# Softmax sums kept per row, heads of batch 0 moved by a quarter, and filler products between quarters of a decode kernel

## The chip, the core and the metric

The kernel runs on one core of a Trainium2 chip. The core's engines work side by side and wait for each other by semaphores: PE (TensorE, matrix products), DVE (VectorE), ACT (ScalarE), POOL (GpSimd) and SP (SyncE, which here only starts DMA transfers). The metric is the device time of one execution in microseconds, lower is better.

## The reference

One decode step of a transformer block for two sequences: layernorm, attention of one query over the last 2048 positions of a cache of 8192 (32 heads of 192), an output projection, and a gated feed-forward.

```python
q = (x_norm @ wq).reshape(B, 1, 32, 192)            # B = 2, D = 640
k = k_cache[:, :, 8192 - 2048:, :]                  # W = 2048 positions
v = v_cache[:, :, 8192 - 2048:, :]
scores = einsum("bhqd,bhkd->bhqk", q, k) * 192 ** -0.5
p = softmax(scores, axis=-1)
o = einsum("bhqk,bhkd->bhqd", p, v)
h = x + o.reshape(B, 1, 6144) @ wo
out = h + (gelu(norm(h) @ w_gate) * (norm(h) @ w_up)) @ w_down
```

All inputs are bf16. K and V of the window are some 100 of the 122 MB that the kernel reads.

## The kernel before

**Blocks and quarters.** K and V come in eight blocks each: block i holds 512 positions of all 32 heads of one batch, 128 partitions of 48 KB, one row for each head and each run of 128 positions (partition 4 h + r). Four blocks make a batch. A block is worked on as two *quarters* g (16 in all, two for each block, eight for each batch); a quarter is 64 positions of each of the 128 rows. Below, the two quarters of one block are called a pair, counted from 0 to 7.

**Memory.** A ring in SBUF has three slots of 48 KB a partition: two for K (blocks in turn) and one for V. SP issues in one order: wq, K0, V0, K1, V1, K2 and so on, then the four parts of wo and the feed-forward weights. Each issue waits until what lay in its place has been used: V of pair i+1 waits for the last PV product of pair i, and K of pair i+2 stands behind it in SP's queue.

**One pair (loop at the end of the kernel; `emit_loop` writes it as a hardware loop over J of four trips, two pairs a trip).**
- `transposes` (L554): K must lie with the head dimension on partitions. PE transposes 128x128 f32 tiles (two bf16 in one f32) in 12 groups of 4 into four PSUM banks `tps`; 7 groups are copied out by DVE (L565), 5 by ACT (L563).
- `scores` (L615): 24 products of 512 columns into the bank `sps`. Each of the 128 output rows holds the scores of one head and one group of positions; four rows make up a head.
- `row_max` and `softmax`: DVE adds a mask and takes each row's maximum (L625), spreads it by a one-hot row into `mrhs`; PE multiplies by the permutation `pm` (L633) so that each row sees the maxima of the four rows of its head; DVE reduces these to the negated maximum `nms` (L635); ACT takes the exponential with its row sums `zr` (L637).
- `e_blocks`: DVE transposes the weights in 32x32 blocks and places them (L647, L649); `pv`: 64 products with V (L661); DVE copies the result to `osb` (L670).
- The transposes of the second quarter stand in PE's queue before and after the first quarter's L633.
- After two pairs: `weights` (minimum of the stored `nms`, factors `wz` by ACT, L643) and `combine` (PE product with `rowsel`, L678; DVE joins the four `osb` and the older sum into `osum`, L684).
- `heads_done(b)` divides by the sum, spreads `osum` over the columns by f32 products with `colsel` (L695) and brings the heads into the layout for the output projection. For batch 0 it runs inside the loop after J = 1, behind pair 3; for batch 1 after the loop, followed by `oproj` (L718) and the feed-forward.

Every engine takes its instructions in program order. PE's order inside the loop is therefore that of the calls:

```python
                scores(g + 1)
                e_blocks(g)
                row_max()
                softmax(g + 1)
                if g % 4 == 2:
                    weights()
                e_blocks(g + 1)
                pv(g)
                pv(g + 1)
            combine()
            if J == 1:
                P.loop_seg("op", J)
                heads_done(0)
```

Of the kernel before, what the change touches and what calls it, by code (L numbers as in the profile page):

```python
# [6 lines left out]
F32 = mybir.dt.float32  # L7
I32 = mybir.dt.int32
# [219 lines left out]


GRAN = 256  # L230
SLOT = 49152
RING = 3 * SLOT
TPG = 128
# [3 lines left out]
BIG = 1.0e9  # L237
# [9 lines left out]
def bass_sequential_preLN__sliding_block_cached__geglu_ffn__decode_kernel(  # L247
# [12 lines left out]
    with ExitStack() as ctx:  # L260

        def sb(name, shape, dt):
            return ctx.enter_context(nc.sbuf_tensor(name, shape, dt))
# [8 lines left out]
        identf = sb("identf", [128, 128], F32)  # L272
        onesd = sb("onesd", [128, 128], F32)
        pm = sb("pm", [128, 128], BF16)
        rowsel = sb("rowsel", [128, 128], F32)
        colsel = sb("colsel", [128, 512], F32)
        mska = sb("mska", [128, 32], F32)
        oht = sb("oht", [128, 4], F32)
# [7 lines left out]
        pf = sb("pf", [128, 9], F32)  # L286
        pg = sb("pg", [128, 14], F32)
        ci = sb("ci", [128, 128], I32)
        cf = sb("cf", [128, 3, 128], F32)
        ei = sb("ei", [128, 6], I32)  # L290
        ef = sb("ef", [128, 6], F32)
        ge = sb("ge", [128, 6, 5], F32)
# [16 lines left out]
        qrow = sb("qrow", [128, 2, 2, DH], BF16)  # L309
        rq = sb("rq", [128, 6, 4, 32], BF16)  # L310
        qs = sb("qs", [128, 384], BF16)
        mx = sb("mx", [128, 1], F32)
        mrhs = sb("mrhs", [128, 4], BF16)
        sm = sb("sm", [128, 512], F32)
        gate = sb("gate", [128, 1], F32)
        nms = sb("nms", [128, 5], F32)
        nmin = sb("nmin", [128, 1], F32)
        zr = sb("zr", [128, 5], F32)
        z5 = sb("z5", [128, 5], F32)
        wz = sb("wz", [128, 6], F32)  # L320
        wp = sb("wp", [128, 6], F32)
        rinv = sb("rinv", [128, 1], F32)
        eexp = sb("eexp", [128, 512], BF16)
        et = sb("et", [128, 512], BF16)
        eblk = sb("eblk", [128, 2, 16, 4, 32], BF16)
        osb = sb("osb", [128, 4, DH], F32)
        osum = sb("osum", [128, DH], F32)
        onrm = sb("onrm", [128, DH], F32)
        cti = eexp[:, :].bitcast(I32).rearrange("p (k x) -> p k x", k=2)
        cxi = ktr[:, 0, :].bitcast(I32)[:, 0:512]  # L330
        cxf = ktr[:, 1, :].bitcast(F32)[:, 0:512]
        ot32 = sb("ot32", [128, 24], F32)
# [78 lines left out]

        def dve(fn, R=(), W=(), X=(), cls=1):
            return P.op("dve", fn, R, W, X, cls=cls if looped else 0)

        def act(fn, R=(), W=(), X=(), cls=0):
            return P.op("act", fn, R, W, X, cls=cls)

        def pe(fn, R=(), W=(), X=(), cls=0):
            return P.op("pe", fn, R, W, X, cls=cls)

        def pool(fn, R=(), W=(), X=()):
            return P.op("pool", fn, R, W, X)

        def ts(out, in0, s1, op0, s2=None, op1=None):
            def fn(e):
                kw_ = {"op1": op1} if op1 is not None else {}
                return e.tensor_scalar(out=out, in0=in0, scalar1=s1, scalar2=s2, op0=op0, **kw_)  # L427
            return fn
# [73 lines left out]
            k = BITS.index(m)  # L502
            return pf[:, k:k + 1]

        for k, pat in enumerate(([[4, 32], [0, 4]], [[0, 4], [1, 32]])):
            pool(lambda e, k=k, pat=pat: e.iota(cti[:, k, :], pattern=pat, base=0, channel_multiplier=0), W=[("cti", k)])
        pool(lambda e: e.tensor_copy(cf[:, 1:3, :], cti[:, :, :]), R=[("cti", k) for k in range(2)], W=["cfm"])

        pool(ts(pg[:, 4:5], rb(28), rb(96), ALU.add), R=["pf"], W=["p124"])
        pool(ts(pg[:, 5:6], rb(3), rb(12), ALU.add), R=["pf"], W=["p15"])  # L510
# [17 lines left out]
        pool(lambda e: e.memset(osum[:, :], 0.0), W=["osum"])  # L528

        def consts_late():  # L530
            pool(ts(rowsel[:, :], cf[:, 2, :], 4.0, ALU.mult, pg[:, 4:5], ALU.is_equal), R=["cfm", "p124"], W=["rowsel"])
            pool(ts(mask16[:, :], cf[:, 0, 0:16], pg[:, 5:6], ALU.is_equal), R=["cf0", "p15"], W=["mask16"])
            pool(lambda e: e.iota(cxi, pattern=[[1, 32], [0, 16]], base=0, channel_multiplier=0), W=["cxi"], X=["ktrc"])
            pool(lambda e: e.tensor_copy(cxf, cxi), R=["cxi"], W=["cxf"])
            pool(ts(colsel[:, :], cxf, rb(31), ALU.is_equal), R=["cxf", "pf"], W=["colsel"] + [("kt", n) for n in range(12)])
            pool(ts(bsel[:, :], cf[:, 0, 0:2], rb(31), ALU.is_equal, 1.0 / D, ALU.mult), R=["cf0", "pf"], W=["bsel"])
            for h in range(2):
                pool(ts(hsel[:, h, :], cf[:, 0, 0:17], 512.0 * h, ALU.add, pg[:, 12:13], ALU.is_equal), R=["cf0", "c63"], W=[("hsel", h)])
# [81 lines left out]
            if g % 4 == 3 and g + 1 < 4 * NQ:  # L620
                q_masked((g + 1) // 8)

        def row_max():
            dve(lambda e: e.memset(gate[:, :], 0.0), W=["gate"], X=["s"], cls=0)
            dve(lambda e: e.tensor_tensor_reduce(  # L625
                out=sm[:, :].rearrange("p (u x) -> p u x", x=32), in0=sps[:, :].rearrange("p (u x) -> p u x", x=32),
                in1=mska[:, :].unsqueeze(1).to_broadcast([128, 16, 32]), scale=1.0, scalar=-2.0 * BIG, op0=ALU.add, op1=ALU.max,
                accum_out=mx[:, :]), R=["mska"], W=["sm", "mx"], X=["s"], cls=0)
            dve(ts(mrhs[:, :], oht[:, :], mx[:, 0:1], ALU.mult), R=["oht", "mx"], W=["mrhs"], cls=0)

        def softmax(g):
            n = g % 4
            pe(lambda e: e.matmul(m2[:, 256:260], lhsT=pm[:, :], rhs=mrhs[:, :], start=True, stop=True),  # L633
               R=["pm", "mrhs"], X=["m2"])
            dve(lambda e: e.tensor_reduce(out=nms[:, n:n + 1], in_=m2[:, 256:260], axis=AX.X, op=ALU.max, negate=True),  # L635
                W=[("nm", n)], X=["m2"], cls=0)
            act(lambda e: e.activation(out=eexp[:, :], in_=sm[:, :], func=ACT.Exp, bias=nms[:, n:n + 1], scale=1.0,  # L637
                                       accum_out=zr[:, n:n + 1]), R=[("nm", n), "sm", "gate"], W=["eexp", ("zr", n)])

        def weights():  # L640
            dve(lambda e: e.tensor_reduce(out=nmin[:, :], in_=nms[:, :], axis=AX.X, op=ALU.min), R=[("nm", k) for k in range(5)],
                W=["nmin"], cls=0)
            act(lambda e: e.activation(out=wz[:, 0:5], in_=nms[:, :], func=ACT.Exp, bias=nmin[:, 0:1], scale=-1.0),  # L643
                R=["nmin"] + [("nm", k) for k in range(5)], W=["wz"])

        def e_blocks(g):
            dve(lambda e: e.transpose(et[:, :], eexp[:, :]), R=["eexp"], W=["et"], cls=0)  # L647
# [22 lines left out]
            dve(lambda e: e.tensor_copy(osb[:, g % 4, :], bank[:, 0:DH]), W=[("osb", g % 4)], X=[x], cls=0)  # L670

        def combine():
            dve(lambda e: e.tensor_tensor_reduce(out=z5[:, :], in0=wz[:, 0:5], in1=zr[:, :], scale=1.0, scalar=0.0, op0=ALU.mult,
                                                 op1=ALU.add, accum_out=wz[:, 5:6]), R=["wz"] + [("zr", k) for k in range(5)],
                W=["z5", "wz5"], cls=0)
            dve(lambda e: e.tensor_copy(zr[:, 4:5], wz[:, 5:6]), R=["wz5"], W=[("zr", 4)], cls=0)
            dve(lambda e: e.tensor_copy(nms[:, 4:5], nmin[:, :]), R=["nmin"], W=[("nm", 4)], cls=0)
            pe(lambda e: e.matmul(m2[:, 264:270], lhsT=rowsel[:, :], rhs=wz[:, :], start=True, stop=True), R=["rowsel", "wz", "wz5"],  # L678
               X=["m2"])
            dve(lambda e: e.tensor_scalar(out=wp[:, :], in0=m2[:, 264:270], scalar1=0.25, scalar2=None, op0=ALU.mult), W=["wp"],  # L680
                X=["m2"], cls=0)
            dve(ts(osum[:, :], osum[:, :], wp[:, 4:5], ALU.mult), R=["wp", "osum"], W=["osum"], cls=0)
            for k in range(4):
                dve(lambda e, k=k: e.scalar_tensor_tensor(out=osum[:, :], in0=osb[:, k, :], scalar=wp[:, k:k + 1], in1=osum[:, :],  # L684
                                                          op0=ALU.mult, op1=ALU.add), R=["wp", "osum", ("osb", k)], W=["osum"], cls=0)

        def heads_done(b):
            dve(lambda e: e.reciprocal(rinv[:, :], wp[:, 5:6]), R=["wp"], W=["rinv"])
            dve(ts(onrm[:, :], osum[:, :], rinv[:, 0:1], ALU.mult, 0.25, ALU.mult), R=["rinv", "osum"], W=["onrm"])
            dve(lambda e: e.memset(nms[:, 4:5], BIG), W=[("nm", 4)])  # L690
            for y in range(2):
                def fn(e, y=y):
# [44 lines left out]
            pe(fn, R=["hrow", ("hsel", 0), ("hsel", 1)], X=["m2"])  # L737


        consts_late()  # L740
        q_rows()
        q_stationary()
        looped.append(True)
        for J in range(4):
            P.loop_seg("a", J)
            for g in (4 * J, 4 * J + 2):
                transposes(g, 0, 12)
                scores(g)
                row_max()
                transposes(g + 1, 0, 4)  # L750
                softmax(g)
                transposes(g + 1, 4, 12)
                scores(g + 1)
                e_blocks(g)
                row_max()
                softmax(g + 1)
                if g % 4 == 2:
                    weights()
                e_blocks(g + 1)
                pv(g)  # L760
                pv(g + 1)
            combine()
            if J == 1:
                P.loop_seg("op", J)
                heads_done(0)
        P.loop_seg()
        heads_done(1)
        for J in range(4):
# [87 lines left out]
             dma="dout")  # L856


        P.resolve({("dve", 0): 4 * 17 + 10, ("dve", 1): 0, ("dve", 2): 1, ("pe", 2): 1, ("act", 1): 0, ("act", 0): 4 * 6 + 1, ("pool", 0): 4})
        sems = {}  # L860
        for e, c in (("pe", 0), ("pe", 1), ("pe", 2), ("dve", 2), ("act", 0), ("act", 1), ("dve", 0), ("dve", 1), ("pool", 0)):
            sems[e, c] = ctx.enter_context(nc.semaphore(f"s_{e}{c}"))
# [3 lines left out]
        nc.sync.wait_ge(sems["d", "dout"], 16)  # L866
        P.emit("pool", nc.gpsimd, sems)
        P.emit("act", nc.scalar, sems)
        order = ["a", (0, 2, ["op"])]
        P.emit_loop("dve", nc.vector, sems, 4, order)  # L870
        P.emit_loop("pe", nc.tensor, sems, 4, order)

# [27 lines left out]
```

## Time and profile before

| | |
|---|---|
| median of 3 runs | 300.34 us (298.68 to 300.59) |
| profiled execution | 299.82 us, span of its instructions 298.5 us |
| busy: PE, DVE, ACT, POOL | 182.9 us (61%), 154.2 (52%), 93.4 (31%), 22.0 (7%) |
| bytes read from HBM | 122.29 MB, 410 GB/s over the span |
| mean granted PE clock | 0.897 |

The page cuts the span into 40 slices of 7.46 us; a digit is a share in tenths. The granted clock is that share of full speed which PE's clock gate lets through. A line of a timeline gives start, length, engine, line of code, operation, output and inputs, shapes, the count of instructions merged into it, and in brackets the idle time before it with what ended it. A line of the view of stretches gives, for each engine, the busy time and the count of instructions, and at its end the granted clock, the DMA share and GB/s.

### The profile page before, as it was taken

Reading aid. Unit: us, or ns where it says so; the run is one execution under the profiler, and the core shown is the slowest. Engines: PE = TensorE matmul, PEld = TensorE weight load, DVE = VectorE, ACT = ScalarE, POOL = GpSimd, SP = SyncE. Lnnn points to the kernel's source line nnn. Section 1 sums busy time; section 2 is a strip of 40 time slices with the busy share of each in tenths; the row PEclk is TensorE's granted clock in tenths of the full one; section 3 lists DMA queues with packets and bytes.
Section 4 is the critical chain, followed back from the end, with each engine's and each line's share of the span. In section 5 each row is a group of like instructions: output and inputs, shape, how many; then the busy total and the mean of one; then the engine's idle time right before and its main releaser. Section 6 shows DMA issues by size and latency. Waiting matters only on the chain.

```text
span 298.5 us, 6292 instructions
## 1 busy us (share of the span) xinstructions
PE 182.9 (61%) x2573; PEld 148.7 (50%) x2573; DVE 154.2 (52%) x387; ACT 93.4 (31%) x124; POOL 22.0 (7%) x67
## 2 busy tenths in 40 slices
PE   2007088629852985298539864994278628862685
PEld 1006087418732973197338743872277418742352
DVE  5000046735675567256766683667446724676413
ACT  1001036405630563046302550662046404640001
POOL 8910200000020000000200000002000000000000
PEclk9999759997998799869995999799879986999589
DMA  8999999999999999999999998999999989999990
GB/s 317 493 403 417 422 422 422 451 397 448 450 435 411 435 422 429 408 435 428 441 402 422 422 422 336 422 422 422 448 461 441 435 329 415 410 428 432 424 400 32
DMA packets 4203, 122.44 MB, mean 410 GB/s; under 512 B 478, under 2 KB 608, under 8 KB 1248
## 3 DMA queue, kind: packets, MB, share of 16 engines
q1 hardware_dynamic: 4044, 121.90, 96.1%
q10 hardware_dynamic: 148, 0.40, 0.3%
q8 instruction: 7, 0.11, 0.1%
q14 instruction: 4, 0.03, 0.0%
HBM read 122.29 MB, written 0.00 MB: 410 GB/s over the span
## 4 chain that ended last, share of the span: by engine, by line
DMA 55%; PE 24%; DVE 9%; ACT 6%; issue 3%; SPq 1%; DVEq 0%; ACTq 0%
DMA ring<-in_A_k_cache_dram 48%; PE tpp L554 13%; DMA ring<-in_A_wq_dram 7%; ACT ktr L563 4%; DVE eblk L649 2%; PE sps L615 2%; PE m L661 2%; ACT eexp L637 2%; DVE et L647 2%; PE m L718 2%; PE tpp L577 2%; PE sps L695 1%; DVE ktr L565 1%; DVE sm L625 1%; SPq L371 1%
## 5 line engine op out<-in xcount | busy, mean ns | idle before, releaser
L554 PE MATMUL tpp<-identf,ring 128*128 128x128 f32 x768 | 105.5, 303 | 38.4 <-DMA ring<-in_A_k_cache_dram 37.7
L554 PEld LDWEIGHTS tpp<-identf,ring 128*128 128x128 f32 x768 | 97.9, 157 | 46.9 <-DMA ring<-in_A_k_cache_dram 38.8
L563 ACT ACTIVATE ktr<-tpp 128x1024 bf16<-128x1024 bf16 x80 | 77.5, 1026 | 120.9 <-PE tpp L554 120.9
L565 DVE COPY ktr<-tpp 128x1024 bf16<-128x1024 bf16 x112 | 75.3, 689 | 62.5 <-PE tpp L554 61.4
L615 PE MATMUL sps<-ktr,rq 128*32 128x512 bf16 x384 | 25.2, 390 | 13.8 <-DVE ktr L565 13.8
L615 PEld LDWEIGHTS sps<-ktr,rq 128*32 128x32 bf16 x384 | 10.0, 94 | 24.2 <-ACT ktr L563 17.5
L431 POOL TENSOR_TENSOR rq<-qs,mask 128x192 bf16<-128x192 bf16 x16 | 7.7, 514 | 182.3 <-PE sps L615 168.4
L637 ACT ACTIVATE eexp<-sm,nms 128x512 bf16<-128x512 f32 x16 | 11.6, 723 | 29.1 <-DVE nms L635 29.1
L661 PE MATMUL m<-ring,eblk 128*32 128x192 bf16 x512 | 12.2, 248 | 13.3 <-DVE eblk L649 13.3
L649 DVE COPY eblk<-et 32x512 bf16<-32x512 bf16 x64 | 18.2, 285 | 2.1
L661 PEld LDWEIGHTS m<-ring,eblk 128*32 128x32 bf16 x512 | 10.4, 108 | 15.1 <-DVE eblk L649 15.1
L625 DVE CUSTOM_DVE_ANT_1 sm<-sps,mska 128x512 f32<-128x512 f32 x16 | 11.0, 691 | 7.4 <-issue 7.0
L577 PE MATMUL tpp<-ring,xnT 128*32 128x192 bf16 (+1 forms) x112 | 5.2, 371 | 15.4 <-DMA ring<-in_A_wq_dram 15.4
L647 DVE STREAM_TRANSPOSE et<-eexp 128x512 bf16<-128x512 bf16 x16 | 11.3, 706 | 6.3 <-ACT eexp L637 6.3
L577 PEld LDWEIGHTS tpp<-ring,xnT 128*32 128x32 bf16 x112 | 4.1, 133 | 16.2 <-issue 15.5
L661 PE MATMUL ops<-ring,eblk 128*32 128x192 bf16 x512 | 12.2, 248 | 0.0
L600 DVE CAST qs<-ops 128x384 bf16<-128x384 f32 x1 | 0.6, 558 | 21.3 <-PE ops L595 21.3
L695 PE MATMUL sps<-onrm,colsel 128*128 128x192 f32 x16 | 6.6, 566 | 7.3 <-DVE nms L690 6.0
L661 PEld LDWEIGHTS ops<-ring,eblk 128*32 128x32 bf16 x512 | 10.4, 108 | 0.1
L633 PE MATMUL m<-mrhs,pm 128*128 128x4 bf16 x16 | 2.8, 173 | 11.8 <-DVE mrhs L427 11.8
L633 PEld LDWEIGHTS m<-mrhs,pm 128*128 128x128 bf16 x16 | 1.5, 96 | 15.9 <-DVE mrhs L427 15.9
L695 PEld LDWEIGHTS sps<-onrm,colsel 128*128 128x128 f32 x16 | 4.5, 324 | 8.5 <-DVE nms L690 6.1
(131 smaller groups left out, 94.1 us busy)
## 6 DMA issues: line engine op xcount, KB each, us to landing
ring<-in_A_k_cache_dram SPq DMA_DIRECT2D x8, 6144.0 KB, 34.1
ring<-in_A_v_cache_dram SPq DMA_DIRECT2D x8, 6144.0 KB, 20.1
ring<-in_A_wq_dram SPq DMA_DIRECT2D x1, 7680.0 KB, 21.8
ring<-in_A_wo_dram SPq DMA_DIRECT2D x4, 1920.0 KB, 26.6
ring<-in_B_w_gate_dram SPq DMA_DIRECT2D x1, 1536.0 KB, 21.0
ring<-in_B_w_up_dram SPq DMA_DIRECT2D x1, 1536.0 KB, 24.2
ring<-in_B_w_down_dram SPq DMA_DIRECT2D x1, 960.0 KB, 19.8
ring<-in_B_w_down_dram SPq DMA_DIRECT2D x1, 480.0 KB, 20.6
```

The lines of the kernel that those rows point to most:

```text
L431: return lambda e: e.tensor_tensor(out=out, in0=a, in1=b, op=op)
L554: ins = e.transpose(bank[:, 128 * u:128 * (u + 1)], kv[:, off:off + 128], identf[:, :])
L563: act(lambda e, dst=dst, src=src: e.activation(out=dst, in_=src, func=ACT.Copy), W=[("kt", n)], X=[x])
L565: dve(lambda e, dst=dst, src=src: e.tensor_copy(dst, src), W=[("kt", n)], X=[x], cls=0)
L577: ins = e.matmul(tps[0][32 * r:32 * (r + 1), u:u + n], lhsT=xnT[:, c, 32 * J:32 * (J + 1)], rhs=wq[:, c, o:o + n], start=(c == 0 and J == ...
L615: ins = e.matmul(sps[32 * hg:32 * (hg + 1), :], lhsT=rq[:, k, hg, :], rhs=cols, start=(k == 0), stop=(k == 5), tile_position=(0, 32 * hg))
L625: dve(lambda e: e.tensor_tensor_reduce(out=sm[:, :].rearrange("p (u x) -> p u x", x=32), in0=sps[:, :].rearrange("p (u x) -> p u x", x=32) ...
L637: act(lambda e: e.activation(out=eexp[:, :], in_=sm[:, :], func=ACT.Exp, bias=nms[:, n:n + 1], scale=1.0, accum_out=zr[:, n:n + 1]), R=[(" ...
L647: dve(lambda e: e.transpose(et[:, :], eexp[:, :]), R=["eexp"], W=["et"], cls=0)
L649: dve(lambda e, hg=hg: e.tensor_copy(eblk[32 * hg:32 * (hg + 1), g % 2, :, hg, :], et[32 * hg:32 * (hg + 1), :].rearrange("p (a x) -> p a ...
L661: ins = e.matmul(bank[32 * r:32 * (r + 1), 0:DH], lhsT=eblk[:, g % 2, a, :, :].rearrange("p s x -> p (s x)")[:, r:128:4], rhs=vv[:, DH * t ...
L695: ins = e.matmul(sps[:, DH * j:DH * (j + 1)], lhsT=colsel[:, 128 * J:128 * (J + 1)], rhs=onrm[:, :], start=True, stop=True, skip_group_che ...
```

## The change

Four things are altered.

- **Own maximum and sums for each row.** A quarter's softmax no longer asks for the maximum of its head. DVE negates the masked scores and takes the row's minimum straight into `nms`, and ACT takes the exponential with it. So the rows of a head have different offsets.
- **Rows joined once per two pairs.** `maxima` (before the second quarter's `e_blocks`) takes the smallest `nms` of a row over the quarters and the older sum, and the factors `wz`. `sums` (between the two PV products) multiplies by `pm` for the head's common maximum, gives each row its factor `wz[:, 5]` to it, and joins the sums. `combine` has two PE products, a permutation `rowperm` for the factors and `rowsum` for the sum over the rows of a head.
- **Heads of batch 0.** `heads_done(0)` is called after pair 4 (g = 8) instead of after pair 3. The loop's body has a second part for it, "b".
- **Filler.** `keep_busy` is called once in each pair, after `pv(g + 1)` and `combine`. It issues 11 f32 products of `rowsum` with `sm` (128x512) into the bank `tps[3]`; nothing reads what they write.

```diff
+FILL = 11
...
-        def row_max():
+        def softmax(g):
+            n = g % 4
             dve(lambda e: e.memset(gate[:, :], 0.0), W=["gate"], X=["s"], cls=0)
             dve(lambda e: e.tensor_tensor_reduce(
...
-                in1=mska[:, :].unsqueeze(1).to_broadcast([128, 16, 32]), scale=1.0, scalar=-2.0 * BIG, op0=ALU.add, op1=ALU.max,
-                accum_out=mx[:, :]), R=["mska"], W=["sm", "mx"], X=["s"], cls=0)
-            dve(ts(mrhs[:, :], oht[:, :], mx[:, 0:1], ALU.mult), R=["oht", "mx"], W=["mrhs"], cls=0)
+                in1=mska[:, :].unsqueeze(1).to_broadcast([128, 16, 32]), scale=-1.0, scalar=2.0 * BIG, op0=ALU.add, op1=ALU.min,
+                accum_out=nms[:, n:n + 1]), R=["mska"], W=["sm", ("nm", n)], X=["s"], cls=0)
+            act(lambda e: e.activation(out=eexp[:, :], in_=sm[:, :], func=ACT.Exp, bias=nms[:, n:n + 1], scale=-1.0,
+                                       accum_out=zr[:, n:n + 1]), R=[("nm", n), "sm", "gate"], W=["eexp", ("zr", n)])
+
+        def maxima():
+            dve(lambda e: e.tensor_reduce(out=nmin[:, :], in_=nms[:, :], axis=AX.X, op=ALU.min), R=[("nm", k) for k in range(5)],
+                W=["nmin"], cls=0)
+            dve(ts(mrhs[:, :], oht[:, :], nmin[:, 0:1], ALU.mult), R=["oht", "nmin"], W=["mrhs"], cls=0)
+            act(lambda e: e.activation(out=wz[:, 0:5], in_=nms[:, :], func=ACT.Exp, bias=nmin[:, 0:1], scale=-1.0),
+                R=["nmin"] + [("nm", k) for k in range(5)], W=["wz"])
+
+        def sums():
             pe(lambda e: e.matmul(m2[:, 256:260], lhsT=pm[:, :], rhs=mrhs[:, :], start=True, stop=True),
                R=["pm", "mrhs"], X=["m2"])
...
+            dve(lambda e: e.tensor_reduce(out=nmh[:, :], in_=m2[:, 256:260], axis=AX.X, op=ALU.min), W=["nmh"], X=["m2"], cls=0)
+            act(lambda e: e.activation(out=wz[:, 5:6], in_=nmin[:, :], func=ACT.Exp, bias=nmh[:, 0:1], scale=-1.0),
+                R=["nmin", "nmh"], W=["wz5"])
+            dve(lambda e: e.tensor_tensor_reduce(out=z5[:, :], in0=wz[:, 0:5], in1=zr[:, :], scale=1.0, scalar=0.0, op0=ALU.mult,
+                                                 op1=ALU.add, accum_out=zsum[:, :]), R=["wz"] + [("zr", k) for k in range(5)],
+                W=["z5", "zsum"], cls=0)
+            dve(lambda e: e.tensor_copy(zr[:, 4:5], zsum[:, :]), R=["zsum"], W=[("zr", 4)], cls=0)
+            dve(lambda e: e.tensor_copy(nms[:, 4:5], nmin[:, :]), R=["nmin"], W=[("nm", 4)], cls=0)
+            dve(tt(wz[:, 6:7], wz[:, 5:6], zsum[:, :], ALU.mult), R=["wz5", "zsum"], W=["wz6"], cls=0)
...
         def combine():
...
-            pe(lambda e: e.matmul(m2[:, 264:270], lhsT=rowsel[:, :], rhs=wz[:, :], start=True, stop=True), R=["rowsel", "wz", "wz5"],
-               X=["m2"])
...
+            def fn(e):
+                e.matmul(m2[:, 264:270], lhsT=rowperm[:, :], rhs=wz[:, 0:6], start=True, stop=True)
+                return e.matmul(m2[:, 270:271], lhsT=rowsum[:, :], rhs=wz[:, 6:7], start=True, stop=True)
+
+            pe(fn, R=["rowperm", "rowsum", "wz", "wz5", "wz6"], X=["m2"])
...
+        def keep_busy():
+            def fn(e):
+                for k in range(FILL):
+                    ins = e.matmul(tps[3][:, :], lhsT=rowsum[:, :], rhs=sm[:, :], start=True, stop=True)
+                return ins
+
+            pe(fn, R=["rowsum", "sm"], X=[("t", 3)])
...
                 transposes(g, 0, 12)
                 scores(g)
-                row_max()
-                transposes(g + 1, 0, 4)
                 softmax(g)
-                transposes(g + 1, 4, 12)
+                transposes(g + 1, 0, 12)
                 scores(g + 1)
                 e_blocks(g)
-                row_max()
                 softmax(g + 1)
                 if g % 4 == 2:
-                    weights()
+                    maxima()
                 e_blocks(g + 1)
                 pv(g)
+                if g % 4 == 2:
+                    sums()
                 pv(g + 1)
-            combine()
-            if J == 1:
-                P.loop_seg("op", J)
-                heads_done(0)
+                if g % 4 == 2:
+                    combine()
+                keep_busy()
+                if g == 8:
+                    P.loop_seg("op", J)
+                    heads_done(0)
+                if g % 4 == 0:
+                    P.loop_seg("b", J)
...
-        order = ["a", (0, 2, ["op"])]
+        order = ["a", (1, 3, ["op"]), "b"]
```

`heads_done` itself now scales `osum` by one factor per row, `wfin`, which `combine` has made from `rowsum`'s sum and the row's own factor.

## The prediction

> **What bounds the kernel now.** I read the slices of the page first, then the chain that ended last, then the DMA issues of SP and the PE timeline where a K block lands. The slices:
>
> ```profile
> PEclk9999759997998799869995999799879986999589
> DMA  8999999999999999999999998999999989999990
> GB/s 317 493 403 417 422 422 422 451 397 448 450 435 411 435 422 429 408 435 428 441 402 422 422 422 336 422 422 422 448 461 441 435 329 415 410 428 432 424 400 32
> ```
>
> DMA is busy nearly always, so up to the last block the time is that of moving K and V: 12.6 MB a pair of quarters. K blocks are detected on PE at 67.75, 97.61, 126.68, then 186.21, 217.96 and 247.19. The shortest steps are 29.1 and 29.2 us, the longest 31.7: SP issues the next V only when the pair's last PV product is done (212.4 us of SP's waiting is for L661), and where that came late DMA ran dry. From the timelines of SP and PE:
>
> ```profile
> 183.47 0.54 SPq L371 DMA_DIRECT2D ring<-in_A_v_cache_dram  x1
> ...
> 210.65 0.54 SPq L371 DMA_DIRECT2D ring<-in_A_v_cache_dram  x1
> ...
> 186.21 4.07 PE L554 MATMUL tpp<-identf,ring 128*128 128x128 f32 x20 [2.79 <-DMA ring<-in_A_k_cache_dram]
> ...
> 217.96 4.31 PE L554 MATMUL tpp<-identf,ring 128*128 128x128 f32 x25 [6.30 <-DMA ring<-in_A_k_cache_dram]
> ```
>
> At 183.47 only 2.8 us were left before K landed; the slice around it fell to 336 GB/s and the next K came 31.7 us later. At 210.65, 7.3 us were left and the next step took 29.2. So PE idles 2.8 to 7.3 us between pairs. That idle time is the whole budget of the filler.
>
> One pair takes, from the first transpose to the last PV product, 24.1 us (67.75 to 91.86). I cut it at PE's marks: transposes of the first quarter until its scores 7.8 (67.75 to 75.52), scores 1.5, transposes of the second 6.75 (77.05 to 83.80), scores to the end of PV 8.06. The first part runs at half clock, in the view of stretches:
>
> ```profile
> 67.75:70.60 2.85, 2.85 (x14) 2.85 (x15) 0.69 (x1) 0.85 (x1) 0.00 (x0) 0.50 0.72 310
> 70.60:75.50 4.90, 4.06 (x36) 3.70 (x34) 4.05 (x6) 4.06 (x5) 0.00 (x0) 1.00 1.07 461
> 126.68:132.00 5.32, 5.32 (x25) 5.32 (x26) 2.08 (x3) 2.05 (x2) 0.00 (x0) 0.50 1.00 425
> ```
>
> The third figure from the end is the granted clock. The other pairs begin with 2.8 to 5.3 us at 0.50.
>
> **The filler.** One call is 11 f32 products of 128x512, queued on PE behind the pair's last PV product and ahead of the next pair's first transpose. The trace has no such shape. The nearest rows are the f32 products of L695 and the f32 transposes, each asked for inside one stretch:
>
> ```profile
> L695 PE MATMUL sps<-onrm,colsel x3: 527/527/527, 276.3 to 276.9; 128*128 128x192 f32 x3
> ...
> L554 PE MATMUL tpp<-identf,ring x10: 421/421/421, 68.2 to 70.1; 128*128 128x128 f32 x10
> ...
> L554 PE MATMUL tpp<-identf,ring x15: 272/273/394, 70.4 to 72.0; 128*128 128x128 f32 x15
> ```
>
> L695 stands with 16 records for 8 products in the code, so one f32 product is two records. Their starts lie 0.32 us apart (three starts in 0.6 us) for 192 columns at clock 0.50, that is 1.67 ns a column. The transposes confirm it and show the other clock: 1.9/9 = 0.21 us for 128 columns at 0.50 (1.65 ns a column), 1.6/14 = 0.11 at 1.00, half. So 512 columns cost 0.853 us a record at 0.50 and 0.427 at 1.00. The filler starts right after PV, where the clock stands at 1.00 (it fell only at 94.5, 2.6 us after the last PV record), and is itself dense, so I take 1.00: 22 x 0.427 = **9.4 us a call**, eight calls, 75 us of PE. The ends: with a weight load of 0.188 us (L678's f32 load at full clock) between records 13.5 us; all at half clock 18.8; at one record a product 4.7. The loads of L695 lie beside the products (each starts with the record before it, and 0.337 us of load fits a spacing of 0.32), so I take 9.4.
>
> The Trainium skill, "FP8 and Floating Point Precision", section TensorE Precision Notes, gives true FP32 four passes through the array, which is what two records of two cycles a column amount to. "Perfetto Trace Analysis", section Engine Utilization, halves the array's rate for one FP32 form; by that a call would be 4.7 us. The record count of L695 stands with the first.
>
> **What the filler warms.** The next transposes follow it at once, at full clock. In the first part 2.85 us at 0.21 held 13.4 transposes, which at 0.11 take 1.4 us: about 1.45 us saved. PE then is no longer its limit: seven DVE copies of 0.69 and five ACT copies of 1.02 on four banks give some 6.3 us, the same saving. (The second quarter's transposes, warm, took 6.75 with softmax work between.)
>
> **Own maximum for each row.** Removed per quarter: mrhs (0.23 to 0.53), PE product L633 (0.18), nms reduction (0.16) and their hand-overs. In the second quarter they are on the path:
>
> ```profile
> 86.33 0.08 DVE L625 DVE_READ_ACCUMULATOR2_ANT mx<- 128x1 f32 x1
> 86.45 0.53 DVE L427 TENSOR_SCALAR mrhs<-oht,mx 128x4 bf16<-128x4 f32 x1
> ...
> 87.44 0.72 ACT L637 ACTIVATE eexp<-sm,nms 128x512 bf16<-128x512 f32 x1 [3.82 <-DVE nms L635]
> ```
>
> The exponential moves from 87.44 to about 86.48: 0.96 us saved. In the first quarter it frees nothing: e_blocks still stands behind the last of the seven DVE copies, and the exponential, now ahead of ACT's first copy instead of its third, delays that copy to about 1.7 us after the first transpose (before 1.2); ACT's 0.72 + 5 x 1.0 us ends as before. I add 0.1. Pair: 24.1 - 1.45 - 0.95 + 0.1 = **21.8 us**.
>
> **maxima, sums, combine.** nmin and mrhs (0.16 + 0.23) lie under the exponential (0.72 + 0.19). The small DVE steps of sums (some 0.9 us by the rows of 0.14 to 0.17) lie under the second PV product (1.52). combine now has four f32 PE records instead of two; with weight loads of 0.19 they hold PE 0.7 us ahead of the filler, after pairs 1, 3, 5 and 7. Its DVE work (3 us) lies under the filler. The two added POOL steps (about 1 us) have ended long before the first scores at 46.
>
> **Heads of batch 0.** They move behind the filler of pair 4 (pairs counted from 0). Before, they delayed pair 4: products 155.88 to 159.81, transposes only from 159.60. At full clock I take 2.4 us of PE (two times 0.85, plus 0.57 and hand-overs), plus 1.0 for the DVE steps (0.57 + 0.82 + 0.18) that then stand ahead of the first copies: 3.4 us. The loop's new branches lie under the filler.
>
> **The sum.** Pair 0 starts at 38.25 as before and still cold; its PV ends at 63.1 - 1.0 = 62.1. Each further pair begins when the filler ends, since K lands earlier: at worst the K after next landed 34.5 us after a pair's end before (183.47 to 217.96), while PE now asks for it 9.5 + 21.8 + 9.5 us after. So PE sets the period, 21.8 + 9.5 = 31.3 us against 29.1. Last PV: 62.1 + 7 x 31.3 + 3 x 0.7 + 3.4 = 286.7, before 271.68.
>
> Tail: heads_done(1)'s first product started 4.1 us after the last PV; now 0.7 + 9.4 + 0.1 = 10.2 after, the DVE work being long ready: 296.9. From there the old tail took 22.7 (275.78 to 298.5). At a warm clock two times 0.75 go from the products and perhaps 1.0 from oproj, whose 5.25 us ran at 0.65 on average. 296.9 + 20.2 = 317.1 span. The profiled execution took 299.82 for a span of 298.5, and lay 0.5 under the median of 300.34; with its 1.3 us: **318 us**. With F for one filler, the span is 241.9 + 8 F as long as PE sets the period; it meets the old one at F = 7.1.
>
> **Rivals.**
> - *The filler fits (faster).* One record a product, F = 4.7: the pair is 26.6 us, DMA sets 29.1, no pair comes late again (K of pair 7 at 67.7 + 6 x 29.1 = 242.3 instead of 247.2), last PV 264.1, tail 25.7: span 290, 291 us. For it: the idle time of 4.6 to 7.3 us has room for 4.7. Against it: 16 records for 8 products. It decides wherever F is under 7.1. Chance 0.08.
> - *Near the old time:* pair and filler together about 29 us, each some 1.2 us shorter than I have them: 297 to 303. 0.03.
> - *The weight loads don't overlap* (13.5 a call: 351 us) or the clock is cut to half in the dense products (18.8: 394 us). Against both: L695's loads; no stretch of dense PE work before shows under 1.00 once warm. 0.06 together.
> - The forecast holds 0.83. Its own spread: a filler record by the transposes' warm spacing with its bank waits (0.467) adds 7; a pair 0.8 shorter and nothing for heads and combine takes away 10.
>
> The range 308 to 326 leaves out the rivals. Within 1% is what a measurement here can't tell from no change. Faster 0.09, same 0.03, slower 0.88.
>
> **What would show it.** Right: PE busy without a break from PV to the next transposes, in 22 records spaced 0.43; no PE wait for K after pair 0; granted clock 1.00 from 43 us on; K steps of about 31.5 us; DMA with gaps, under 400 GB/s; SP's V issues at about 62, 93, 125, 156. Wrong: filler records at another spacing (F enters eight times), PE waits for K of some us in each pair, or a pair that isn't 21.8 us because copies, not PE, hold its first part.

## The result and the profile after

The changed kernel takes 325.47 us against 299.86 (medians of six runs each). The ratio is 1.088, with a 95% interval of 1.080 to 1.095; this ratio and those below leave out executions more than 1.5% longer than the fastest of their kernel. The forecast was slower, 318 us, with 308 to 326 as its range. The ratio on the 300.34 us that the forecast started from gives 326.6, just over the range. So the direction and the bound were right and the size was too small: 18 us foretold, 25 to 26 measured. The single executions took 324.0 to 331.7 us at mean granted clocks of 0.963 to 0.937; the shortest has the highest clock, but the order is not strict (325.0 us at 0.945, 326.0 at 0.953). The profiled one is the shortest; its span is 322.6 us against 317.1 foretold.

The slices of the changed kernel's page:

```profile
PE   1015288798869887988798869886998599869685
PEclk9999589999999997999999979999999979999989
DMA  9899999999999996999799979995799979899900
GB/s 372 384 458 404 457 408 453 411 451 420 435 374 392 402 469 281 402 402 463 305 402 390 463 293 396 408 463 219 292 463 414 390 305 475 385 430 422 406 18 2
```

PE's row has risen, and DMA's row has holes, the deepest a slice of 219 GB/s. The chain that ended last says the same by engine, 56% PE and 12% DMA where it was 24% and 55%:

```profile
PE 56%; DVE 13%; DMA 12%; issue 12%; ACT 7%; DVEq 0%; SPq 0%
PE tpp L753 25%; PE tpp L559 22%; DMA ring<-in_A_k_cache_dram 12%; PE m L673 4%; DVE eblk L661 4%; ACT eexp L635 4%; DVE et L659 4%; ACT ktr L568 2%; DVE sm L631 2%; PE m L728 2%; DVE ot L712 1%; PE sps L705 1%; DVE sm L435 1%; DVE ktr L570 0%; PE sps L820 0%
```

L753 is the filler, a quarter of the span on the chain. PE's timeline around the first filler, and SP's issues of V, which mark the ends of pairs 0 to 4:

```profile
62.53 9.71 PE L753 MATMUL tpp<-sm,rowsum 128*128 128x512 f32 x22
72.08 5.51 PE L559 MATMUL tpp<-identf,ring 128*128 128x128 f32 x48
```

```profile
62.64 0.54 SPq L375 DMA_DIRECT2D ring<-in_A_v_cache_dram  x1
...
94.81 0.53 SPq L375 DMA_DIRECT2D ring<-in_A_v_cache_dram  x1
...
127.42 0.53 SPq L375 DMA_DIRECT2D ring<-in_A_v_cache_dram  x1
...
159.52 0.54 SPq L375 DMA_DIRECT2D ring<-in_A_v_cache_dram  x1
...
191.96 0.53 SPq L375 DMA_DIRECT2D ring<-in_A_v_cache_dram  x1
```

22 records hold PE from 62.53 to the next transpose at 72.08, with no idle time in between and no wait for K. The pair's steps are 32.2, 32.6, 32.1 and 32.4 us where 31.3 or 32.0 were foretold.

**Where the rest came from.** The half-clock stretches of the loop have become fewer, but are not gone; they have moved from the start of a pair to its end. The clock fell at 125.31, 190.17 and 258.43 us. In the view of stretches, the 3.41 us ahead of each fall, and after two of them what followed:

```profile
121.90:125.31 3.41, 1.21 (x63) 1.00 (x56) 2.32 (x8) 0.82 (x2) 0.00 (x0) 1.00 1.04 449
124.90:127.30 2.40, 2.37 (x64) 2.08 (x64) 0.36 (x1) 0.00 (x0) 0.00 (x0) 0.59 0.05 21
127.30:129.00 1.70, 1.70 (x7) 0.87 (x4) 0.36 (x1) 0.00 (x0) 0.00 (x0) 0.58 1.01 347
186.76:190.17 3.41, 1.22 (x61) 1.00 (x56) 2.21 (x6) 0.79 (x2) 0.00 (x0) 1.00 1.00 432
255.02:258.43 3.41, 1.22 (x60) 1.22 (x64) 2.21 (x6) 0.12 (x2) 0.00 (x0) 1.00 0.53 231
258.80:262.10 3.30, 3.30 (x8) 1.50 (x5) 0.36 (x1) 0.00 (x0) 0.00 (x0) 0.54 0.71 238
```

The first figure after the length is PE's busy time, the third from the end the granted clock. Ahead of each fall PE was busy 1.2 us of 3.41: the window holds the whole idle time of 2.2 us between the two groups of PV products, and on one or both sides of it some of these products. What followed, PV products and the first filler records, ran at a granted clock of 0.54 to 0.59 on average. PE's timeline for pair 2:

```profile
121.22 1.52 PE L673 MATMUL ops<-ring,eblk 128*32 128x192 bf16 x64 [0.22 <-DVE eblk L661]
124.93 2.46 PE L673 MATMUL m<-ring,eblk 128*32 128x192 bf16 x64 [2.20 <-DVE eblk L661]
127.32 10.39 PE L753 MATMUL tpp<-sm,rowsum 128*128 128x512 f32 x22
```

That is 2.46 us instead of 1.52, and 10.39 instead of 9.71. In the kernel before, the idle time here was 1.67 us, and a window of 3.41 us around it held 1.75 us of PE work; the clock stayed at 1.00. Its timeline in pair 1 and the view of stretches in pair 2:

```profile
90.33 1.52 PE L661 MATMUL m<-ring,eblk 128*32 128x192 bf16 x64 [1.67 <-DVE eblk L649]
```

```profile
118.39:121.80 3.41, 1.75 (x79) 1.34 (x68) 2.10 (x6) 0.00 (x0) 0.00 (x0) 1.00 0.83 360
```

With own maxima the first PV product no longer stands behind L633 and starts earlier (at once after `e_blocks`), so the gap grew by half a microsecond.

### The profile page after: what moved, and what is told of

The parts are those of the page before. It is cut to its first block, busy times and chain, and to the rows that moved or that the text cites. A ratio compares the mean times of both kernels' runs of the same rounds, so it can differ in the third digit from the quotient of the medians.

```text
span 322.6 us, 6609 instructions
## 1 busy us (share of the span) xinstructions
PE 247.5 (77%) x2745; PEld 169.9 (53%) x2745; DVE 151.0 (47%) x373; ACT 94.7 (29%) x128; POOL 22.9 (7%) x69
## 4 chain that ended last, share of the span: by engine, by line
PE 56%; DVE 13%; DMA 12%; issue 12%; ACT 7%; DVEq 0%; SPq 0%
PE tpp L753 25%; PE tpp L559 22%; DMA ring<-in_A_k_cache_dram 12%; PE m L673 4%; DVE eblk L661 4%; ACT eexp L635 4%; DVE et L659 4%; ACT ktr L568 2%; DVE sm L631 2%; PE m L728 2%; DVE ot L712 1%; PE sps L705 1%; DVE sm L435 1%; DVE ktr L570 0%; PE sps L820 0%
## 5 line engine op out<-in xcount | busy, mean ns | idle before, releaser
L570 DVE COPY ktr<-tpp 128x1024 bf16<-128x1024 bf16 x112 | 76.6, 690 | 80.9 <-PE tpp L559 79.6
L568 ACT ACTIVATE ktr<-tpp 128x1024 bf16<-128x1024 bf16 x80 | 76.6, 1018 | 118.9 <-PE tpp L559 118.9
L559 PE MATMUL tpp<-identf,ring 128*128 128x128 f32 x768 | 92.8, 280 | 11.8 <-DMA ring<-in_A_k_cache_dram 8.9
L559 PEld LDWEIGHTS tpp<-identf,ring 128*128 128x128 f32 x768 | 85.7, 143 | 23.0 <-DMA ring<-in_A_k_cache_dram 9.0
L753 PE MATMUL tpp<-sm,rowsum 128*128 128x512 f32 x176 | 80.6, 615 | 0.0
L753 PEld LDWEIGHTS tpp<-sm,rowsum 128*128 128x128 f32 x176 | 34.1, 198 | 41.0 <-issue 40.9
L673 PE MATMUL m<-ring,eblk 128*32 128x192 bf16 x512 | 14.3, 269 | 17.7 <-DVE eblk L661 17.1
L673 PEld LDWEIGHTS m<-ring,eblk 128*32 128x32 bf16 x512 | 11.9, 115 | 19.1 <-DVE eblk L661 18.3
L435 DVE TENSOR_TENSOR sm<-sps,mask 128x384 f32<-128x384 f32 x4 | 2.2, 558 | 17.8 <-PE sps L705 17.8
L682 DVE COPY osb<-m 128x192 f32<-128x192 f32 x8 | 2.9, 358 | 10.2 <-PE m L673 10.2
## 6 DMA issues: line engine op xcount, KB each, us to landing
ring<-in_A_wo_dram SPq DMA_DIRECT2D x4, 1920.0 KB, 23.3
```

Of the source, the lines that this page charges most:

```text
L435: return lambda e: e.tensor_tensor(out=out, in0=a, in1=b, op=op)
L559: ins = e.transpose(bank[:, 128 * u:128 * (u + 1)], kv[:, off:off + 128], identf[:, :])
L568: act(lambda e, dst=dst, src=src: e.activation(out=dst, in_=src, func=ACT.Copy), W=[("kt", n)], X=[x])
L570: dve(lambda e, dst=dst, src=src: e.tensor_copy(dst, src), W=[("kt", n)], X=[x], cls=0)
L673: ins = e.matmul(bank[32 * r:32 * (r + 1), 0:DH], lhsT=eblk[:, g % 2, a, :, :].rearrange("p s x -> p (s x)")[:, r:128:4], rhs=vv[:, DH * t ...
L753: ins = e.matmul(tps[3][:, :], lhsT=rowsum[:, :], rhs=sm[:, :], start=True, stop=True)
```

## The experiments

All expectations were written before the runs. Times are medians with the kernel before on the same chip beside them (298.7 to 300.2).

### Without the filler

```diff
-                keep_busy()
```

> The changed kernel without its filler; the rest of the change stays. Theory A (the filler alone makes PE set the period; own rows and the moved heads gain a little): DMA sets the period again, steps between K blocks near 29.2 us with one late pair behind the heads of batch 0, last PV at about 268, 297 us (295 to 300). Rival B (the new softmax order, the joins or the split loop cost time too): more than 302 us, with a pair longer than 23.2 us from first transpose to last PV. Every pair should again begin with 2.8 to 5.3 us at clock 0.50.

296.36 us, 0.991 of the kernel before (0.986 to 0.996), as theory A has it. All that the change does besides the filler is a gain of about 1%; the whole loss appears only with the filler.

### FILL 5

```diff
-FILL = 11
+FILL = 5
```

> FILL 5 instead of 11: 10 records of 0.43 us, 4.4 us a call. Theory A: pair and filler together are 26.2 us, under the 29.1 of DMA, so only the tail pays for a call (about 1 us) and gets it back from a warm clock; no late pair but the one behind the heads: 292 us (289 to 296). Rival C (each call costs its length wherever PE stands, since the filler keeps products or copies from starting): run without filler plus 8 x 4.4 = 35 us, about 332. Rival D (the filler's warmth is worth nothing where DMA sets the period): as the run without filler within 2 us.

294.78 us, 0.988 (0.976 to 0.999). Calls of 4.6 us add nothing to the run without them, so a call does not cost its length (rival C, 332 us, is out). DMA is full again until the tail, and PE waits for K. In the timeline:

```profile
118.76 4.56 PE L753 MATMUL tpp<-sm,rowsum 128*128 128x512 f32 x10
126.09 4.07 PE L559 MATMUL tpp<-identf,ring 128*128 128x128 f32 x20 [2.78 <-DMA ring<-in_A_k_cache_dram]
```

The interval touches rival D too: what the warmth is worth where DMA sets the period is under 2 us here. It took 2.8 us more than the 292 expected, most of it in the tail: 27.9 us from the last PV product to the end, where the forecast's tail (30.4 us with F = 9.4) gives 25.4 for F = 4.4. The last call took 6.36 us instead of 4.56 and the output projection 5.01, both with the clock down for a part of them.

### The kernel before with the filler alone

```diff
+        def keep_busy(n=11):
+            def fn(e):
+                for k in range(n):
+                    ins = e.matmul(tps[3][:, :], lhsT=rowsel[:, :], rhs=sm[:, :], start=True, stop=True)
+                return ins
+            pe(fn, R=["rowsel", "sm"], X=[("t", 3)])
...
                 pv(g + 1)
+                if g % 4 == 0:
+                    keep_busy()
             combine()
+            keep_busy()
```

> The kernel before with nothing but 11 f32 products of rowsel with sm behind each pair. Theory A: pair 24.1 - 1.45 = 22.7 us plus 9.5, period 32.2, last PV at about 295, span 327, 328 us: slower than the changed kernel by some 3 us, because the own rows (0.95 us a pair) are missing. PE idles only 1.67 us between the two PV products here, so the clock should hold 1.00 from 44 us to the tail. Rival B (own rows cost time): equal to the changed kernel or faster.

327.2 us (one run), foretold 328. So the filler alone does the harm to the old kernel too. The stretch that covers the loop:

```profile
44.00:292.00 248.00, 204.65 (x2323) 141.53 (x2322) 135.31 (x326) 85.90 (x114) 5.81 (x12) 1.00 0.92 392
```

The clock is at 1.00 throughout, with the idle time of 1.67 us between the PV products: the half clock of the changed kernel goes with the longer gap. By the medians the changed kernel is 1.7 us faster than this one, where some 3 were expected. In the next run, whose clock holds, it is 8.3 us faster: that is what the rest of the change is worth here, against a single execution, and the half clock takes 6.5 us of it back.

### Two products between the PV products, 11 behind

```diff
                     sums()
+                keep_busy(2)
                 pv(g + 1)
```

> The changed kernel with two more filler products (1.7 us) between the two PV products, where PE idles 2.1 to 2.2 us; the 11 behind the pair stay. Theory E (the clock fell to 0.50 at 125, 190 and 258 us because a window of PE held little work around that idle time, and this cost some 5 us in slow PV products and slow filler records): no stretch at 0.50 between 44 us and the tail, and 319 to 321 us, faster than the changed kernel although PE has 13 products a pair instead of 11. Rival F (the clock falls for another reason, such as dense f32 products or DMA standing still): still three or more stretches at 0.50 and 324 us or more.

318.94 us, 1.066 (1.055 to 1.076). PE does two products more in each pair and the kernel is 6.5 us *faster* than the changed one, as theory E has it. The same place in pairs 2 and 4, in the view of stretches (pair 6 has the same figures):

```profile
118.90:126.50 7.60, 7.07 (x158) 4.26 (x159) 4.99 (x15) 0.82 (x2) 0.00 (x0) 1.00 0.89 383
182.00:189.50 7.50, 7.00 (x157) 4.20 (x158) 4.96 (x16) 0.82 (x2) 0.00 (x0) 1.00 0.74 321
```

PE is busy 7.0 us of 7.5 and the clock holds; in this trace it does not fall between 44 us and the tail. The steps between pair ends are 31.3 to 31.7 us (34.2 with the heads), the 31.3 to 32.0 of the forecast (34.7), and the time is its 318.

### 11 products in bf16

```diff
-                    ins = e.matmul(tps[3][:, :], lhsT=rowsum[:, :], rhs=sm[:, :], start=True, stop=True)
+                    ins = e.matmul(tps[3][:, :], lhsT=pm[:, :], rhs=eexp[:, :], start=True, stop=True)
```

> The changed kernel with 11 filler products of the same shape in bf16 (permutation pm with the exponentials) instead of f32. Theory A (the price is records times columns: an f32 product is two records of 0.43 us): 11 records of 0.22 us, 2.4 us a call, under the idle time, so DMA sets the period: 294 to 297 us. Rival I (the price is per product whatever its type): 9.5 us a call, 324 us.

295.2 us (one run). The price of a product depends on its type:

```profile
120.51 2.32 PE L753 MATMUL tpp<-eexp,pm 128*128 128x512 bf16 x10 [0.16 <-issue]
125.90 2.40 PE L559 MATMUL tpp<-identf,ring 128*128 128x128 f32 x10 [3.07 <-DMA ring<-in_A_k_cache_dram]
```

A product in bf16 is one record, and these start some 0.22 us apart, where a product in f32 is two records 0.43 us apart. A call is some 2.4 us instead of 9.7 (the trace holds 10 of its 11 records), and PE waits 3.07 us for K behind it.

### Heads of batch 0 back behind pair 3, no filler

```diff
-                keep_busy()
-                if g == 8:
-                    P.loop_seg("op", J)
-                    heads_done(0)
-                if g % 4 == 0:
-                    P.loop_seg("b", J)
+            if J == 1:
+                P.loop_seg("op", J)
+                heads_done(0)
...
-        order = ["a", (1, 3, ["op"]), "b"]
+        order = ["a", (0, 2, ["op"])]
```

> The changed kernel without filler and with the heads of batch 0 back behind pair 3. Theory A (moving the heads only moves the late pair by one): as the run without filler, 296 us within 1.5, the slow step now from the pair that starts near 159 us. Rival J (the move itself is a gain): 2 to 3 us slower than the run without filler, 298 to 300.

296.81 us, 0.993 (0.988 to 0.997), against 296.36 with the heads moved: no difference that can be measured. The gain of 1% without filler belongs to the own rows. Moving the heads moves the late pair: the longest step between the starts of pairs is the one from 126.06 to 156.63 us here, and the one from 186.07 to 217.11 in the profile without filler.

### FILL 8

```diff
-FILL = 11
+FILL = 8
```

> FILL 8: 6.9 us a call. Theory A (two bounds: DMA's 29.1 us a pair below F of about 7, PE's 21.8 + F + 0.1 above): pair and filler 28.8 us, so DMA still sets the period and only the tail grows by 2.6 us against the run with 5: 297 us (295 to 300). Rival C (the time grows evenly with the filler): halfway between the runs with 5 and 11, 310 us.

Its four executions took 302.1, 304.7, 310.4 and 311.3 us, at mean granted clocks of 0.960, 0.943, 0.921 and 0.921. None lies in theory A's range, and only the two with the lowest clock lie near rival C's 310. In the profiled one (302.1) the clock fell twice at the same place, with the filler behind it:

```profile
89.30:91.50 2.20, 2.20 (x65) 1.90 (x65) 0.85 (x7) 0.29 (x1) 0.00 (x0) 0.66 0.94 402
92.30:101.50 9.20, 9.20 (x18) 3.94 (x19) 2.31 (x8) 0.00 (x0) 0.00 (x0) 0.75 1.06 454
...
216.60:223.50 6.90, 6.90 (x18) 3.07 (x18) 2.31 (x9) 0.00 (x0) 0.00 (x0) 1.00 0.87 349
```

The 16 filler records take 9.2 us there and 6.9 at full clock. This run could not tell an even rise from the two bounds plus the clock, so the next one held the clock.

### Two between, 8 behind

The diff is that of the run with two products between, with `FILL = 8`.

> Two filler products between the PV products and 8 behind the pair. The run with 8 behind the pair and none between took 302 to 311 us where two bounds alone gave 297; in its profile the clock stood at 0.50 for two times 6.8 us, at PV and filler. Theory E (the two bounds hold, and the rest is the half clock): with the clock held, pair and filler 28.9 us, 297 us (295 to 300), and no stretch at 0.50 between 45 us and the tail. Rival C (the time grows evenly with the filler, whatever the clock): 302 us or more, as two more products a pair are issued.

298.85 us, 0.994 (0.989 to 1.000). That is theory E: the time lies under the 302 of the run before it although 16 products more are issued. The loop and the tail:

```profile
45.00:268.00 223.00, 201.41 (x2305) 138.26 (x2305) 132.65 (x314) 87.56 (x117) 5.81 (x12) 1.00 1.00 427
268.00:294.60 26.60, 19.57 (x252) 11.22 (x252) 9.88 (x34) 1.27 (x4) 0.00 (x0) 1.00 0.79 328
```

DMA share and clock are at 1.00 over the whole loop: with 28.9 us expected for pair and filler, DMA's 29.1 is still the period. So with the clock held the time is nearly flat up to a filler of about 7 us. Beyond it, from 8 products behind the pair to 11, it rises by 20.1 us (298.85 to 318.94) for 2.6 us of F: about 8 for each microsecond, as in the forecast's sum.

### A version faster than both

```diff
-                keep_busy()
+                keep_busy(5 if g % 4 == 0 else 3)
...
+            if J < 3:
+                P.loop_seg("kb", J)
+                keep_busy(2)
...
                 pe(fn, R=["colsel", "onrm"], X=["s"])
+                if b == 1:
+                    tail_busy(1, 256) if y == 0 else tail_busy(2, 512)
...
-        order = ["a", (1, 3, ["op"]), "b"]
+        order = ["a", (1, 3, ["op"]), "b", (None, 3, ["kb"])]
```

`keep_busy(n)` issues n products, in all 5 behind each pair and 3 behind the last; `tail_busy(n, w)` issues n products of `rowsum` with w columns of `colsel`.

> The changed kernel with 5 filler products behind each pair but only 3 behind the last, and fillers in PE's idle time inside the heads of batch 1: one of 256 columns after the first pair of products, two of 512 after the second. Theory G (the tail of the run with 5 products, 27.9 us after the last PV, is long because the filler holds back the heads by 1 us and the clock falls to 0.50 during the output projection): last PV at 265 as there, first heads product 4.0 us after it, the clock at 1.00 through the output projection, which then takes 3.5 us instead of 5.2: tail 24 us, 290 us (288 to 292). Rival H (fillers in the tail only stand in the way, the clock falls anyway): 294 to 297.

292.75 us, 0.982 (0.973 to 0.991). In the tail the fillers lie in PE's idle time, and the output projection (L730) runs at full clock. In the timeline:

```profile
266.61 2.82 PE L755 MATMUL tpp<-sm,rowsum 128*128 128x512 f32 x6
...
272.00 1.88 PE L763 MATMUL tpp<-colsel,rowsum 128*128 128x512 f32 x4
...
274.21 3.43 PE L730 MATMUL m<-ring,ot 128*2 128x320 bf16 x96
```

The projection takes 3.43 us instead of 5.01, and it is 24.8 us from the last PV product to the end instead of 27.9. That is theory G for the tail, though the last PV product ended at 266.2 and not 265, and the time is 0.75 us over the range expected for it.

With `keep_busy(2)` between the PV products as well:

> The kernel with 5 products behind a pair, 3 behind the last and fillers inside the last heads, with two more products between the PV products. Theory E: no half clock at PV, last PV at 264 instead of 266.3, 290 us (288.5 to 292). Rival K (where DMA sets the period the clock at PV doesn't matter): as without them, 292.7, within 1.

292.45 us, 0.979 (0.971 to 0.986). The last PV product ended at 263.8, as theory E had it, but the time is rival K's: in this profile the tail took 27.1 us, at a mean clock of 0.77, and gave the 2.4 us back. The two traces show what ended both tails. The last products of the feed-forward wait for the last part of its weights, which lands at the same time in both. In the timelines of the run without and of the run with products between:

```profile
288.13 0.70 PE L882 MATMUL m<-ring,uT 128*17 128x160 bf16 x12 [0.41 <-DMA ring<-in_B_w_down_dram]
...
288.04 0.72 PE L883 MATMUL m<-ring,uT 128*17 128x160 bf16 x12 [0.20 <-DMA ring<-in_B_w_down_dram]
```

The issue of these weights stands behind the last PV product, so it came 2.4 us earlier with the products between; but the transfer then took 23.3 us instead of 21.0. So DMA sets the time to the end here, and PV products that end earlier gain nothing.

## Why the prediction came out as it did

**Right: what bounds.** DMA's period of 29.1 us stands against PE's pair and filler; the filler is over the limit; K is never waited for after the first pair.

**Right: the price of a record.** 0.43 us was foretold; the 22 records take 9.55 us from the first to the next transpose (62.53 to 72.08). A product costs four times as much as in bf16, by the run with bf16 products.

**Right: the pair.** 21.8 us was foretold; it is 21.9 in pairs whose clock held (137.55 to 159.47, 269.85 to 291.73). The exponential starts 2.65 us after the scores instead of 3.64, the warm transposes take 6.4 us instead of 7.8. The joins hold PE 0.4 us after the last PV product, not 0.7; the heads of batch 0 cost 3.0 us, not 3.4.

**Wrong: the filler at clock 1.00 and nothing lost at PV.** The step said that the filler starts where the clock stands at 1.00 and bounded the half clock only for the filler as a whole (18.8 us a call), and it foretold 1.00 from 43 us on. I took PV's clock from a trace with an idle time of 1.67 us and did not ask what the shorter softmax does to that idle time. Measured in the profiled execution, the second group of PV products in pairs 2, 4 and 6 is longer by 0.94, 0.77 and 0.16 us, and the filler calls behind them by 0.68, 0.85 and 1.48: in sum 4.9 of the 5.5 us that were missing. That the gap at PV is the cause is shown by filling it: in the run with two products between, the loss is gone.

**The rest.** Pair 1 loses 0.84 us, where the second group of PV products pauses; the profile puts it down to no other engine:

```profile
94.50 0.28 PE L673 MATMUL m<-ring,eblk 128*32 128x192 bf16 x2 [0.57 <-issue]
```

It comes in the loop's first trip alone; its cause was not tried. In the tail the output projection was to gain 1.0 us and gained 0.15 (5.10 us): the clock fell at 306, after 1.8 us without a product. Pair 0 ended at 62.6 us, 0.5 later than I took. Against these stand the joins and the heads, 1.3 us cheaper than foretold, and the last heads, whose first product came 9.9 us after the last PV product instead of 10.2. With the 4.9 us these parts make up the 5.5.

**The rivals.** A filler that fits was the right picture with another number of products: at 5 a call the kernel is faster than before. The weight loads lie beside the products, 0.19 us each in a spacing of 0.43. The reason given for it was weak, since 0.337 us of load does not fit a spacing of 0.32 as the text has it. Dense products did not lower the clock: it stood at 1.00 over the whole loop of the kernel before with the filler.

## What to carry to other kernels

Filler on an in-order engine is free only up to the idle time that the other bound leaves, and from there each microsecond is paid once a trip: count it in records and columns at the clock at hand, f32 at four times bf16, before choosing its number. Put it into the gap where the clock would fall, not behind work that is dense already. And when a step gets shorter, look at what the freed time does to the gaps around it: here half a microsecond more of idle PE in a pair took back 6.5 of the 8.3 us that the rest of the change won beside the filler.

## What the runs showed of the hardware

The clock of PE fell with an idle time of only 2.2 us, where the 3.41 us ahead of the fall held 1.2 us of product records, and did not fall where they held 1.75 (one place of the kernel before). The Trainium skill, "TensorE: Matmul & The Clock Gate", section "HAM oscillation — how this bites in real kernels", warns of idle gaps over some 3.4 us; the measurement is stricter than that.

All falls of the changed kernel's trace last 3.41 us or a multiple of it (the last is cut off by the end), and all begin a multiple of 3.41 us apart: from 125.31 to 190.17 it is 19 times, from there to 258.43 it is 20 times. This grid decides which pairs are hit. In pairs 2, 4 and 6 the whole gap of 2.2 us lies in one window of the grid. In the other five it is split between two, and the emptiest window there, in pair 3, held 1.49 us; the clock stayed at 1.00 behind it:

```profile
156.03:159.44 3.41, 1.49 (x65) 1.34 (x65) 2.61 (x12) 0.34 (x2) 0.00 (x0) 1.00 0.53 231
```

In the loop of the kernel before with the filler, where the gap is 1.67 us, the emptiest window of the grid held 1.54 us, and the clock did not fall there. The other traces agree: on their grids, in the loops of all twelve, the clock fell after each full-clock window with at most 1.38 us of product records and after none with 1.49 or more; of three windows in between, one was followed by a fall. That the grid also makes the spread between executions was not shown, since only one execution of the changed kernel was traced.
